# Two attention products made in column halves with 65 moving columns

## The chip, the cores and the metric

The kernel runs on one core of a Trainium2 chip. Its time is the device time of one execution in microseconds (us), and the median of the runs is what counts. The core has five engines: TensorE (PE, which loads a stationary operand of weights and then streams moving columns through the array), VectorE (DVE), ScalarE (ACT), GpSimd (POOL) and SyncE (SP, which issues most DMAs). In the profile, PEld is TensorE's loading of weights.

## The reference

Attention with random features over four batches, eight heads, 576 positions and 64 dimensions, then two feed-forward layers. The change touches the first part alone:

```python
def phi(x):
    proj = np.einsum('bhsd,md->bhsm', x, omega)      # 128 features
    h = proj - np.sum(x * x, axis=-1, keepdims=True) / 2.0
    h = h - np.max(h, axis=-1, keepdims=True)
    return np.exp(h) / np.sqrt(m)
q_p, k_p = phi(q_s), phi(k_s)
kv  = np.einsum('bhsm,bhsd->bhmd', k_p, v)           # values by features
z   = np.sum(k_p, axis=2)
num = np.einsum('bhsm,bhmd->bhsd', q_p, kv)          # numerators
den = np.einsum('bhsm,bhm->bhs', q_p, z)[..., None] + 1e-06
attn = num / den
...
x = (silu(xn @ w_gate) * (xn @ w_val)) @ w_out       # 512 -> 1536 -> 512, xn: attn after an RMS norm
h = x @ w_in
out = (h * np.cos(h)) @ w_out2                       # 512 -> 2048 -> 512
```

## The kernel before

The 2304 tokens are 18 tiles of 128. A batch has four and a half of them, so tiles 4 and 13 are mixed: half of their tokens belong to one batch and half to the next (`parts`, L84).

**Keys.** For a tile, `project` (L419) multiplies the keys of eight heads by omega: contraction over 64 dimensions, two heads side by side in two row halves of the array (L426). `features` (L430) takes the maximum on DVE (L435) and eight exponentials on ACT (L437). `kv_product` (L577) then adds, for each head, features times values: stationary are the 128 features of 128 tokens, moving are 128 columns, of which 64 are the head's values and 64 are ones from an extra block of the tile `v` (slot `H` of `vt`, set by a memset). So the sum of the features, `z`, comes out beside the values. Of the 128 result columns, `keep_kv` (L597) takes 65. A mixed tile is done in two parts of 64 tokens, one after the other, each into its batch's bank.

**Queries.** A query tile goes through eight steps (`query_step`, L707): projection and features; step 1, `transposed` (L440) and `keep_transposed`; step 2, `sums` (L457), the numerators, and `quotients` (L469); then norm, a transpose and a split in a high and a low part. `sums` has the transposed features stationary and 128 columns of `kv` moving, of which 65 are used. A mixed tile needs the sums of two batches: there the stationary operand is cut in two column halves of 64 tokens, and each half gets its own batch's `kv`, with 128 moving columns each.

All these products are fp32. The array runs each fp32 product of the program as two passes, so that one product has two records of a matmul and two of a weight load in the profile. A tile's eight heads are 16 records.

**What sets the order.** The order is written out by hand, in slots. Slot s does, on each engine in this order, what `older` (L765) lists for it and `begin` (L771) adds. In the first stage, up to about 88.8 us, the slots hold 18 key tiles and six query tiles; the weights of the feed-forward layers are prepared in between on ACT, DVE and POOL (`Weights`, L127; `tick`, L363). In the second stage, up to about 262 us, the other twelve query tiles are woven into the first third of the first layer (fp32r products, L831 and L884), and from then on there are feed-forward products only. ACT, DVE and POOL run their lists in the order written too; SP issues the loads of keys, queries, values (L575) and of raw weights, most of them in one queue. The tile `v` has three buffers: the values of tile t + 3 are asked for when tile t's product has been made (L748).

Of the kernel before, what the change touches and what calls it, by code (L numbers as in the profile page):

```python
# [33 lines left out]
F32 = mybir.dt.float32  # L34
# [10 lines left out]
P = 128  # L45
# [11 lines left out]
def attention_then_ffn(ctx: ExitStack, tc: tile.TileContext, qT, kT, v, omT, wc1, rms_g, wc2, out, B, H, S, D):  # L57
    nc = tc.nc
    M = omT.shape[1]
# [12 lines left out]
    C1, C2 = 3, 2  # L72
    RING = 20
    IDLE = 9
    KVW = H * (D + 1) + D
    G = 4
    GROUPS1 = [range(0, 4), range(4, 8), range(8, 12)]
    PER_PAIR = 7
# [5 lines left out]
    def parts(t):  # L84

        pr, i = divmod(t, TPP)
        if i == MIX:
            return [(2 * pr, 0, P // 2), (2 * pr + 1, P // 2, P // 2)]
        return [(2 * pr + (i > MIX), 0, P)]
# [11 lines left out]
    def bank(tag, name):  # L101
        if tag == "w":
            tag = "wa" if w_taken[0] % 2 == 0 else "wb"
            w_taken[0] += 1
        return psum.tile([P, 512], F32, tag=tag, name=name, bufs=2)
# [299 lines left out]
    class Attention:  # L405
# [51 lines left out]
        def sums(self, t, r):  # L457

            eT = self.eT.pop((t, r))
            ps = bank(self.tag, f"num_ps{t}_{r}")  # L460
            for h in range(HP):
                for b, p0, n in parts(t):
                    at = (2 * h + r) * (D + 1)
                    nc.tensor.matmul(
                        ps[p0:p0 + n, h * P:(h + 1) * P], eT[:, h, p0:p0 + n], self.kv[b][:, at:at + P],
                        start=True, stop=True, skip_group_check=True)
            self.ps["num", t, r] = ps

# [76 lines left out]
    with tc.manual_schedule():  # L545
# [16 lines left out]

        kv = [ap.tile([P, KVW], F32, name=f"kv{b}", bufs=1) for b in range(B)]
        NV = 3
        values = ExitStack()
        vp = values.enter_context(tc.tile_pool(name="values", bufs=1, side="right", reuse_waits="tile"))
        vt = [vp.tile([P, H + 1, D], F32, name=f"v{i}", bufs=1) for i in range(NV)]
        att = Attention(att_tile, "q", kv)


        acc = {}

        def load_v(t):
            if t < NTILE:
                nc.sync.dma_start(vt[t % NV][:, 0:H], v[t])  # L575

        def kv_product(t, i):  # L577

            b, p0, n = parts(t)[i]
            end = p0 + n + t * P == (b + 1) * S  # L580
            for r in range(2):
                begin = (b, r) not in acc
                if begin:
                    acc[b, r] = bank("kv", f"kv_ps{b}_{r}")
                for h in range(HP):
                    hh = 2 * h + r
                    nc.tensor.matmul(
                        acc[b, r][:, h * P:(h + 1) * P], att.e["k", t, r][p0:p0 + n, h, :],
                        vt[t % NV][p0:p0 + n, hh::H - hh, :],
                        start=begin and h == 0, stop=end, skip_group_check=True)  # L590
                if end:
                    keep_kv(b, r)
            if i == len(parts(t)) - 1:
                for r in range(2):
                    del att.e["k", t, r]

        def keep_kv(b, r):  # L597
            nc.vector.tensor_copy(
                kv[b][:, 0:H * (D + 1)].rearrange("p (h two d) -> p two h d", two=2, d=D + 1)[:, r],
                acc.pop((b, r)).rearrange("p (h c) -> p h c", c=P)[:, :, 0:D + 1])  # L600
# [143 lines left out]
        for s, (nm, t) in tiles.items():  # L744
# [4 lines left out]
            else:  # L749
                for i in range(1, 8):  # L750
                    at = s + i + (s >= SLOTS - 1 or i > 1)
# [7 lines left out]
        def load_ahead(s):  # L759
            at = order.index(s) if s in tiles else -1  # L760
            if at >= 0 and at + AHEAD[0] < len(order) and at + AHEAD[0] not in asked:
                asked.add(at + AHEAD[0])
                att.load(*tiles[order[at + AHEAD[0]]])

        def older(s, *steps):  # L765
            for step in steps:
                for k, f, *args in then.get(s, []):
                    if k == step:
                        f(*args)

        def begin(s):  # L771
            if s in tiles:
                att.project(*tiles[s])
                for r in range(2):
                    att.features(*tiles[s], r)
# [12 lines left out]
        ps = bank("q", "idle_ps")  # L788
        for _ in range(IDLE):
            nc.tensor.matmul(ps[:, 0:NB], zeros[:, 0:P], zeros, start=True, stop=True)  # L790
        for a in vt:
            nc.vector.memset(a[:, H], 1.0)
        for a in kv:
            nc.vector.memset(a[:, H * (D + 1):], 0.0)
        make_identity(nc, ident)
        nc.gpsimd.memset(half_pi, math.pi / 2)
        nc.gpsimd.memset(minus_half, -0.5)
# [2 lines left out]
        for s in range(SLOTS):  # L800
            load_ahead(s)
            if s in (0, 1):
                load_v(s + 1)
                wts.load(s + 1, nc.sync)
            if s == 3:
                att.load_gain()
            older(s, 0, -5)
            begin(s)
            older(s, -7, -6, -4, -3, -2, -1, 1)
            if s:  # L810
                wts.tick(5 if s < 6 else 1 if s < 14 else 4 if s + 1 < SLOTS else 0)

# [44 lines left out]
        def product(blk, f, e):  # L857
            w = wts.get(1, f, e)
            o = bank("w", f"gv_ps{blk}_{f}_{e}")[:, :NB]
            passes(o, [(two(w, slice(kk * P, (kk + 1) * P)), part(blk, kk)) for kk in range(KD)])  # L860
            return o

        def silu(blk, f, ps):
            a = row(F32, f"gv{blk}_{f}")
            nc.scalar.activation(a, ps, AF.Silu)
            return a
# [10 lines left out]
        def out1(g, blk, f, t, first, last, es):  # L877

            if first and es[0] == 0:
                yacc[blk] = [bank_of_sums(f"y_ps{g}_{blk}_{f}_{e}")[:, :NB] for e in range(KD)]  # L880
            w = wts.get(1, f, 2)
            for i, j in ((0, 0), (1, 0), (0, 1)):
                for e in es:
                    nc.tensor.matmul(yacc[blk][e], w[:, i, e * P:(e + 1) * P], t[:, j],  # L884
                                     start=first and i + j == 0, stop=last and j == 1)
            if not last:
                return
            for e in es:
                waits.append((put_away, blk, e, yacc[blk][e]))
# [59 lines left out]
        for n, (g, blk, f, first, last) in enumerate(steps):  # L949
            tail = n >= N1 - G  # L950
            if tail:
                wts.freed = C1 * f
            back = 2.0 if tail else wts.rate_back(C1 * G + 5, N1 - G - n) / 2
            if wts.n_front < 6 * FRONT:
                back = 0.0
            rates = wts.rate(FRONTS_BY_1, N1 - G + 1 - n) / 2 if n <= N1 - G else 0.0, back
            if n < G:
                rates = max(rates[0], 4), rates[1]
            s = SLOTS + 2 * n
            load_ahead(s)  # L960
            older(s, -5)
            ps = product(blk, f, 0)
            a = silu(blk, f, ps)
            older(s, -6, -4, -3, -2, -1)
            begin(s)
            if n >= 1:
                out1(*steps[n - 1][:3], hid[n - 1], *steps[n - 1][3:], (0, 1))
            older(s, 1, 0)
            job(2 if tail else 3)
            wts.pace(rates[0], 0.0)  # L970
            older(s + 1, -7)
            wts.pace(0.0, rates[1])
            job(0 if tail else 3)
            if n > N1 - G and early_names:
                bring(1, 0, early_names.pop(0))
            flush(3)
            load_ahead(s + 1)
            older(s + 1, -5)
            ps = product(blk, f, 1)
            hid[n] = gated(blk, f, a, ps)  # L980
            older(s + 1, -6, -4, -3, -2, -1)
            begin(s + 1)
            if n >= 1:
                out1(*steps[n - 1][:3], hid.pop(n - 1), *steps[n - 1][3:], (2, 3))
            older(s + 1, 1, 0)
            job(2 if tail else 3)
            wts.pace(rates[0], 0.0)
            older(s + 2, -7)
            wts.pace(0.0, rates[1])
            job(0 if tail else 3)  # L990
            flush(3)
            if n == N1 - G:
                assert s + 2 > max(then)
                while len(combined) < 2:
                    job(1)
                combine.close()
                open_between()
                limit[0] = NPAIR
                tp[:] = [combine.enter_context(tc.tile_pool(name="combinations2", bufs=3, reuse_waits="tile")), 3]
                early_names = ["B11", "B21", "T2", "T1", "T4"]  # L1000
            if n >= N1 - G and early_names:
                bring(1, 0, early_names.pop(0))
# [291 lines left out]
        for k, (g, p) in enumerate(pairs):  # L1294
            fs = list(GROUPS1[g])
            start = base + (g - 1) * PER_GROUP
# [133 lines left out]
```

## Time and profile before

| | us |
|---|---|
| three runs | 964.46, 964.47, 966.03 |
| median | 964.47 |
| profiled execution | 963.77 |
| its span | 961.9 |
| PE busy in the span | 949.2 |
| DVE busy | 712.3 |
| ACT busy | 536.9 |
| POOL busy | 416.4 |

The span is the time from the first to the last instruction of the profiled execution, 1.9 us less than its time. A busy PE is not a PE at its peak, since matmul ends are modelled and overlap. The profile's windows show per stretch how long each engine worked; its timeline shows when a block of equal instructions began and how long it took to the end of the last; its list of waits says who ended an engine's idle time.

### The profile page before, as it was taken

How to read it: one execution, taken by the hardware profiler on the slowest of the kernel's cores; microseconds unless marked ns; L12 is line 12 of the kernel's file. 1: busy time of each engine (PE TensorE's matmuls, PEld its weight loads, DVE VectorE, ACT ScalarE, POOL GpSimd, SP SyncE). 2: the span in 40 equal slices, each digit the busy share in tenths (PEclk: the TensorE clock that was granted, in tenths of full speed). 3: DMA queues.
4: the chain of work that ended last, by engine and by line, in shares of the span. 5: the costliest groups of instructions: out<-in, count | busy, mean ns of one | idle time of the engine just before them, and what ended most of it. 6: DMA issues, size and time to landing. Idle time of an engine off the chain costs nothing. (4 is left out here: it accounts for less than half of the span.)

```text
span 961.9 us, 16225 instructions
## 1 busy us (share of the span) xinstructions
PE 949.2 (99%) x5761; PEld 892.0 (93%) x5761; DVE 712.3 (74%) x1163; ACT 536.9 (56%) x1155; POOL 416.4 (43%) x377
## 2 busy tenths in 40 slices
PE   9999999999999999999999999999999999999998
PEld 8998999989999999999999998888888889899897
DVE  5786677778863686577686648997799777786766
ACT  7787776775543524354453545575656565464443
POOL 2133367657944867275764673320244221230000
PEclk9999999999999999999999999999999999999999
DMA  8555178778697898846989794967622758307554
GB/s 313 157 181 187 57 265 293 256 265 263 219 328 291 328 330 295 302 152 197 376 303 377 249 348 152 345 231 271 208 88 79 272 186 303 125 23 269 197 226 162
DMA packets 96082, 227.65 MB, mean 237 GB/s; under 512 B 9728, under 2 KB 45184, under 8 KB 96000
## 3 DMA queue, kind: packets, MB, share of 16 engines
q1 hardware_dynamic: 94704, 222.34, 66.1%
q10 hardware_dynamic: 1296, 4.26, 1.2%
q8 instruction: 46, 0.75, 0.3%
q14 instruction: 36, 0.29, 0.1%
HBM read 156.04 MB, written 70.52 MB: 236 GB/s over the span
## 5 line engine op out<-in xcount | busy, mean ns | idle before, releaser
L1251 PE MATMUL o_ps<-w,o 128*128 128x512 f32 x864 | 226.0, 393 | 0.6 <-DVE o L1054 0.6
L209 POOL TENSOR_TENSOR f<-f,raw 128x512 f32<-128x512 f32 x68 | 94.7, 1393 | 230.3 <-DVE raw L204 184.6
L1251 PEld LDWEIGHTS o_ps<-w,o 128*128 128x128 f32 x864 | 159.7, 188 | 24.5 <-DVE o L1054 1.1
L217 POOL TENSOR_TENSOR w<-b,w 128x512 fp32r<-128x512 f32 x88 | 115.5, 1318 | 135.4 <-ACT w L214 125.6
L831 PE MATMUL gv_ps<-xhl,w 128*128 128x384 f32 x576 | 107.9, 335 | 1.6 <-DVE gv L870 1.1
L831 PEld LDWEIGHTS gv_ps<-xhl,w 128*128 128x128 f32 x576 | 100.5, 188 | 2.1 <-DVE gv L870 1.4
L1150 PE MATMUL y<-t,w 128*128 128x384 f32 x576 | 102.1, 334 | 0.3 <-POOL w L217 0.3
L1150 PEld LDWEIGHTS y<-t,w 128*128 128x128 f32 x576 | 100.0, 188 | 0.6 <-POOL w L217 0.6
L1051 ACT CAST o<-turns 128x384 fp32r<-128x384 f32 x96 | 47.5, 513 | 93.3 <-DVE turns L1232 93.3
L1043 PE MATMUL Xh<-T,w 128*128 128x384 f32 x432 | 87.4, 337 | 1.5 <-ACT h L1196 1.5
L1043 PEld LDWEIGHTS Xh<-T,w 128*128 128x128 f32 x432 | 76.8, 188 | 9.7 <-ACT h L1196 4.0
L1043 PE MATMUL X<-T,w 128*128 128x384 f32 x432 | 80.9, 335 | 0.0
L1043 PEld LDWEIGHTS X<-T,w 128*128 128x128 f32 x432 | 75.3, 188 | 0.5 <-DVE r L1078 0.3
L214 ACT CAST w<-b 128x512 fp32r<-128x512 f32 x88 | 50.5, 580 | 31.2 <-DVE b L274 23.9
L1054 DVE TENSOR_TENSOR o<-turns,o 128x384 fp32r<-128x384 f32 x96 | 59.9, 638 | 8.5 <-ACT o L1051 8.1
L884 PE MATMUL y_ps<-t,w 128*128 128x384 f32 x288 | 60.8, 346 | 0.0
L1017 ACT ACTIVATE turns<-turns,half_pi 128x768 f32<-128x768 f32 (+1 forms) x50 | 45.7, 914 | 22.4 <-DVE turns L1221 22.3
L1043 PE MATMUL Yh<-B,w 128*128 128x384 f32 x288 | 58.0, 336 | 0.0
L1221 DVE SCALAR_TENSOR_TENSOR turns<-turns,r 128x768 f32<-128x768 int32 (+1 forms) x50 | 56.4, 1128 | 1.7
L1232 DVE TENSOR_TENSOR turns<-h,turns 128x768 f32<-128x768 f32 (+1 forms) x50 | 54.8, 1096 | 2.4 <-ACT turns L1017 2.4
L1043 PEld LDWEIGHTS Yh<-B,w 128*128 128x128 f32 x288 | 51.4, 188 | 4.2 <-ACT h L1196 0.4
L190 DVE TENSOR_SCALAR f<-W 128x512 int32<-128x512 int32 x68 | 45.1, 663 | 13.6 <-ACT W L182 6.5
(117 smaller groups left out, 1853.6 us busy)
## 6 DMA issues: line engine op xcount, KB each, us to landing
T<-T_dram SPq DMA_DIRECT2D x48, 768.0 KB, 6.9
raw<-wc SPq DMA_DIRECT2D x60, 512.0 KB, 4.9
B<-yh_dram SPq DMA_DIRECT2D x21, 768.0 KB, 5.7
kept<-f SPq DMA_DIRECT2D x56, 256.0 KB, 5.0
b<-kept SPq DMA_DIRECT2D x56, 256.0 KB, 5.1
B<-x_dram SPq DMA_DIRECT2D x15, 768.0 KB, 6.6
x_dram<-xhl SPq DMA_DIRECT2D x12, 768.0 KB, 5.8
s<-x_dram SPq DMA_DIRECT2D x24, 384.0 KB, 6.3
```

The lines of the kernel that those rows point to most:

```text
L209: nc.gpsimd.tensor_tensor(f32(f), f32(f), rest, op=ALU.add)
L214: nc.scalar.copy(t[:, 0, to], src)
L217: nc.gpsimd.tensor_tensor(t[:, 1, to], src, f32(t[:, 0, to]), op=ALU.subtract)
L831: nc.tensor.matmul(o, w[i], x[j], start=n == 0, stop=n == len(terms) - 1)
L884: nc.tensor.matmul(yacc[blk][e], w[:, i, e * P:(e + 1) * P], t[:, j], start=first and i + j == 0, stop=last and j == 1)
L1043: nc.tensor.matmul(o, w[:, i, c + kk * P:c + (kk + 1) * P], x[:, j, kk], start=begin and n == 0, stop=n == 5, skip_group_check=True)
L1051: nc.scalar.copy(t[:, 0], a)
L1054: engine.tensor_tensor(t[:, 1], a, f32(t[:, 0]), op=ALU.subtract)
L1150: nc.tensor.matmul(acc[e], w[:, i, e * P:(e + 1) * P], t[:, j], start=f == fs[0] and i + j == 0, stop=f == fs[-1] and j == 1)
L1221: nc.vector.scalar_tensor_tensor(r, a, -TWO_PI_LO, b, op0=ALU.mult, op1=ALU.add)
L1232: at(mu, lambda: nc.vector.tensor_tensor(r, h, r, op=ALU.mult))
L1251: nc.tensor.matmul(oacc[blk][j], o[:, x, js], w[:, y], start=first and n == 0, stop=last and n == 2)
```

## The change

Both products are cut in two column halves: for each head, the 128 columns of the stationary operand become two instructions of 64 columns each, which stand one behind the other and write PSUM partitions 0 to 63 and 64 to 127. The moving operand shrinks from 128 to 65 columns: 64 values and one column of ones for the values by features, 65 columns of `kv` for the numerators. For that the tile `v` gets a layout of eight heads of 65 columns, the 65th a one, in place of eight heads of 64 columns and a block of ones. Its load from memory was a run of 2048 bytes for each token; it is now eight runs of 256 bytes, 260 bytes apart in the tile. The padding of `kv` and its memsets are dropped. The steps 2 and 1 of queries change places in three lists.

```diff
-    KVW = H * (D + 1) + D
+    KVW = H * (D + 1)
...
             for h in range(HP):
-                for b, p0, n in parts(t):
-                    at = (2 * h + r) * (D + 1)
+                at = (2 * h + r) * (D + 1)
+                for c in range(2):
+                    half_c = slice(c * P // 2, (c + 1) * P // 2)
+                    b = parts(t)[min(c, len(parts(t)) - 1)][0]
                     nc.tensor.matmul(
-                        ps[p0:p0 + n, h * P:(h + 1) * P], eT[:, h, p0:p0 + n], self.kv[b][:, at:at + P],
+                        ps[half_c, h * P:h * P + D + 1], eT[:, h, half_c], self.kv[b][:, at:at + D + 1],
                         start=True, stop=True, skip_group_check=True)
...
-        vt = [vp.tile([P, H + 1, D], F32, name=f"v{i}", bufs=1) for i in range(NV)]
+        vt = [vp.tile([P, H, D + 1], F32, name=f"v{i}", bufs=1) for i in range(NV)]
...
-                nc.sync.dma_start(vt[t % NV][:, 0:H], v[t])
+                nc.sync.dma_start(vt[t % NV][:, :, 0:D], v[t])
...
                     hh = 2 * h + r
-                    nc.tensor.matmul(
-                        acc[b, r][:, h * P:(h + 1) * P], att.e["k", t, r][p0:p0 + n, h, :],
-                        vt[t % NV][p0:p0 + n, hh::H - hh, :],
-                        start=begin and h == 0, stop=end, skip_group_check=True)
+                    for c in range(2):
+                        half_c = slice(c * M // 2, (c + 1) * M // 2)
+                        nc.tensor.matmul(
+                            acc[b, r][half_c, h * P:h * P + D + 1], att.e["k", t, r][p0:p0 + n, h, half_c],
+                            vt[t % NV][p0:p0 + n, hh, :],
+                            start=begin and h == 0, stop=end, skip_group_check=True)
...
-            nc.vector.memset(a[:, H], 1.0)
-        for a in kv:
-            nc.vector.memset(a[:, H * (D + 1):], 0.0)
+            nc.vector.memset(a[:, :, D:], 1.0)
...
-            older(s, -7, -6, -4, -3, -2, -1, 1)
+            older(s, -7, -6, -4, -3, -1, -2, 1)
...
-            older(s, -6, -4, -3, -2, -1)
+            older(s, -6, -4, -3, -1, -2)
...
-            older(s + 1, -6, -4, -3, -2, -1)
+            older(s + 1, -6, -4, -3, -1, -2)
```

PE in the first stage, around the first numerators (`num_ps` is their bank, `kv_ps` that of the values by features, `qp_ps` and `kp_ps` those of projections; "x4" are four program instructions in a row), before:

```order
L426 MATMUL qp_ps_1_547<-om,qraw_421 128x128
L464 MATMUL num_ps_0_570<-kv_97,eT_0_498 128x128 x4
L464 MATMUL num_ps_1_580<-kv_97,eT_1_505 128x128 x4
L587 MATMUL kv_ps_0_447<-v_105,ke_0_520 128x128 x4
L587 MATMUL kv_ps_1_452<-v_105,ke_1_527 128x128 x4
L426 MATMUL kp_ps_0_602<-om,kraw_465 128x128
```

and after:

```order
L426 MATMUL qp_ps_1_607<-om,qraw_457 128x128
L466 MATMUL num_ps_0_630<-kv_97,eT_0_550 64x65 x8
L466 MATMUL num_ps_1_644<-kv_97,eT_1_557 64x65 x8
L591 MATMUL kv_ps_0_483<-v_105,ke_0_572 64x65 x8
L591 MATMUL kv_ps_1_492<-v_105,ke_1_579 64x65 x8
L426 MATMUL kp_ps_0_678<-om,kraw_517 128x128
```

Nothing moved: each block stands where it stood, with twice as many instructions of half the stationary and about half the moving columns. The exchange of steps 1 and 2 moves nothing anywhere on any engine, since no slot holds both.

SP at the start of the program, before:

```order
L575 DMA v_104<-v 128x512
L416 DMA kraw_137<-kT 128x512
L170 DMA raw_139<-wc 128x1024
L416 DMA kraw_169<-kT 128x512
L575 DMA v_105<-v 128x512
```

and after:

```order
L577 DMA v_104<-v 128x8x64
L416 DMA kraw_137<-kT 128x512
L170 DMA raw_139<-wc 128x1024
L416 DMA kraw_165<-kT 128x512
L577 DMA v_105<-v 128x8x64
```

The loads keep their places in the queue; only the form of the values' load differs.

## Rows read from the trace of the kernel before

**Rows 1.** The page: busy time and share of each engine, and the chain's engines.

```profile
PE 949.2 (99%) x5761; PEld 892.0 (93%) x5761; DVE 712.3 (74%) x1163; ACT 536.9 (56%) x1155; POOL 416.4 (43%) x377
PE 42%; DVE 3%; ACT 1%; issue 1%; DVEq 0%; ACTq 0%
```

**Rows 2.** Busy time by stretch: its length, then engines, clock, DMA share, GB/s.

```profile
10.00:20.00 10.00, 10.00 (x107) 9.27 (x104) 7.59 (x14) 8.64 (x30) 4.16 (x3) 1.00 0.99 355
6.57:88.84 82.27, 81.17 (x829) 74.70 (x825) 63.11 (x130) 69.21 (x232) 24.87 (x24) 1.00 0.67 221
88.84:262.00 173.16, 170.22 (x1223) 164.90 (x1222) 131.73 (x266) 117.27 (x260) 114.34 (x119) 1.00 0.66 225
```

**Rows 3.** Groups by line and form: records | busy us, mean ns | idle before.

```profile
L587 PE MATMUL kv_ps<-v,ke 128*128 128x128 f32 x256 | 33.0, 282 | 0.3 <-ACT ke L437 0.3
L464 PE MATMUL num_ps<-kv,eT 128*128 128x128 f32 x256 | 31.8, 277 | 0.0
L464 PEld LDWEIGHTS num_ps<-kv,eT 128*128 128x128 f32 x256 | 30.4, 191 | 1.1 <-DVE eT L454 0.3 <-ACT eT L452 0.3
L464 PEld LDWEIGHTS num_ps<-kv,eT 128*64 128x64 f32 x64 | 3.5, 136 | 0.4 <-issue 0.2
```

**Rows 4.** PE's timeline: start, length to the last end (both us), what, records.

```profile
19.75 1.83 PE L587 MATMUL kv_ps<-v,ke 64*128 64x128 f32 x15
...
42.50 2.05 PE L464 MATMUL num_ps<-kv,eT 128*128 128x128 f32 x16
44.39 1.95 PE L587 MATMUL kv_ps<-v,ke 128*128 128x128 f32 x16
46.27 1.16 PE L426 MATMUL kp_ps<-om,kraw 64*128 64x128 f32 x16
...
70.09 4.03 PE L587 MATMUL kv_ps<-v,ke 64*128 64x128 f32 x32
74.05 1.16 PE L426 MATMUL qp_ps<-om,qraw 64*128 64x128 f32 x16
...
85.12 1.98 PE L464 MATMUL num_ps<-kv,eT 128*64 128x128 f32 x32
87.03 2.05 PE L587 MATMUL kv_ps<-v,ke 128*128 128x128 f32 x16
```

**Rows 5.** PEld's timeline in two windows that hold a block's first loads.

```profile
32.45 0.30 PEld L464 LDWEIGHTS num_ps<-kv,eT 128*128 128x128 f32 x2
...
85.12 0.20 PEld L464 LDWEIGHTS num_ps<-kv,eT 128*64 128x64 f32 x4
```

**Rows 6.** PE's timeline in the second stage, numerators between fp32r products.

```profile
97.94 1.95 PE L464 MATMUL num_ps<-kv,eT 128*128 128x128 f32 x16
99.64 1.29 PE L884 MATMUL y_ps<-t,w 128*128 128x384 f32 x6
...
107.29 1.95 PE L464 MATMUL num_ps<-kv,eT 128*128 128x128 f32 x16
109.16 1.16 PE L426 MATMUL qp_ps<-om,qraw 64*128 64x128 f32 x16
```

**Rows 7.** Waits from 6.57 to 88.84 us: total us, times, longest.

```profile
ACT ke L437 <- DVE kmx L435: 10.0, 8, 3.9
ACT qe L437 <- DVE qmx L435: 3.3, 4, 1.8
ACT w L214 <- POOL f L209: 3.0, 4, 1.3
...
DVE kmx L435 <- PE kp_ps L426: 5.3, 5, 2.1
DVE qmx L435 <- PE qp_ps L426: 5.2, 3, 3.3
```

**Rows 8.** PE's longest wait from 89 to 270 us.

```profile
PE gv_ps L831 <- DVE gv L870: 1.1, 1, 1.1
```

**Rows 9.** DMA: ACT's queue from 0 to 6 us (packets, MB, share); loads of values; the fifth one.

```profile
q10 hardware_dynamic: 144, 0.07, 3.8%
...
v<-v SPq DMA_DIRECT2D x18, 256.0 KB, 4.2
...
L575 SPq DMA_DIRECT2D v<-v x1: 327/327/327, 12.4 to 12.4; - x1
...
DMA to landing us min/median/max: 5.7/5.7/5.7
```

## The prediction, made before the result was known

> **What bounds the kernel now.** I read the page first, then the windows by stage, then the timeline of PE around the two products, then the waits. PE is busy 99% of the span, no other engine over 74% [rows 1], so an instruction taken from PE is worth its time, unless the stage where it lies has another engine close behind. That is so in the first stage: from 6.57 to 88.84 us, 82.27 us long, PE works 81.17 us and ACT 69.21 [rows 2]. In the second stage, 173.16 us, PE works 170.22, DVE 131.73 and ACT 117.27: PE alone bounds it [rows 2]. After that there are feed-forward products alone, which the change leaves as they are. All kv products and five of the 18 blocks of numerators lie in the first stage, the other 13 in the second.
>
> **What a block costs PE, and what it will cost.** A block of a whole tile is 16 records. The numerators at 42.50 give way to the next block at 44.39, and that one at 46.27 [rows 4]: 1.88 us, or 0.118 us a record. Streaming is not the only thing of that length. Two weight loads of 128 columns take 0.30 us from the first start to the last end, one takes 0.191 [rows 3, 5], so the second starts 0.11 after the first: loading keeps the same pace as streaming. So 65 moving columns alone would win little; the column halves have to halve the loads too.
>
> The trace has a block of that form: the mixed tile's numerators at 85.12, 32 records of 64 stationary and 128 moving columns, which give way after 1.91 us [rows 4]. That is 0.119 us a pair of halves, no more than one whole record: the two halves stream at once. The loads as well: four half loads (two pairs) span 0.20 us, one takes 0.136 [rows 3, 5], so the fourth starts 0.064 after the first. In single file, at half of 0.11 each, it would be 0.165. A pair of loads therefore costs 0.055, and a pair of streams 65/128 of 0.11, 0.056. I take **0.060 us a pair** (0.055 to 0.075; a pair is four PE instructions, and no row shows four handed out steadily in under 0.11).
>
> The Trainium skill speaks against this: its page "TensorE: Matmul & The Clock Gate", section "The mechanism", says that a weight load overlaps a running matmul only where their row groups differ, and column halves share theirs. By that rule the mixed block would be 16 times 0.055 + 0.11, or 2.6 us, and the changed pair 0.11, with nothing won. The 1.91 us above disagrees, so I give it no more than the weight of the first rival.
>
> So a block falls by 16 x (0.118 - 0.060) = 0.93 us, less what the pipeline needs to start and drain, which does not shrink: I take 0.83.
> - First stage, kv of 16 whole tiles: 13.3 us.
> - First stage, kv of two mixed tiles: each has two blocks of 16 records of 64 tokens, one behind the other, 3.96 us for 32 [rows 4]; now 32 pairs, 1.9. Together 4.1 us.
> - First stage, five numerators: 4.2 us. The mixed one is among them, with 0.119 a pair before.
> - Second stage, 13 numerators: these stand between whole products, and a change of tiling has a price. A block of them followed by whole products gives way after 1.70 us, one followed by the row-halved projection after 1.87 [rows 6]: 0.17 a change. The changed block needs 16 x 0.058 + 2 x 0.17 = 1.27. It is eight times followed by a projection (0.60 won) and five times not (0.43): 7.0 us.
>
> PE is freed of 21.6 us in the first stage and 7.0 us in the second.
>
> **What of it shows in the end.** First stage: PE's work would fall to 59.6 us, ACT's stays at 69.2. ACT becomes the bound. It sits idle for 13.1 us there, and that alone can be won. Of it, 9.4 us are waits for DVE's maxima (10.0 + 3.3, less the first 3.9, which ends at 6.57), and 3.0 for POOL [rows 7]. DVE in turn waits 10.5 us for projections [rows 7], which come sooner now, but it also has weight work of its own in front of some maxima. I take two thirds of 9.4: **6 us**, between 3 and 9.4. What is late next is ACT itself, and behind it DVE with 63.11 us.
>
> The values' load takes some of it back. It is not shown in pieces of 256 bytes. DMA is 0.99 busy from 10 to 20 us at 355 GB/s [rows 2], 22.4 bytes a ns for each of 16 engines, so a piece of 2048 takes 91 ns; 512-byte pieces, omega's, take 0.038 x 16 x 6 us / 128 = 28 ns [rows 9]. A straight line through both gives 17.5 ns for 256 bytes; the upper end is 28, as much as for 512. A load of 1024 pieces is 64 an engine: 1.1 to 1.8 us against 0.73, 0.4 to 1.06 more. I take 0.73, the middle. DMA is saturated when the first five are fetched, so it adds up: the fifth is issued at 12.39 and lands 5.7 us later, at 18.1, and PE wants it at 19.75 [rows 4, 9]. With five times 0.73 it lands at 21.7: **2 us** lost (0.3 to 3.6). Later loads have two slots of over 2.5 us each from issue to use, against a median landing of 4.2 [rows 9]; no loss.
>
> On transfers the Trainium skill speaks against the change too: its page "DMA: Bandwidth & Descriptors", section "Specifications", wants 512 bytes or more a piece for full speed and says that smaller ones are read, modified and written back. No row here shows a load of that size; by that rule the sum is near that of the third rival.
>
> Second stage: 7.0 us freed. PE waits little there, its longest wait is 1.1 us for DVE [rows 8], but DVE works 76% and will have less room: I take 70%, **5 us** (3 to 7). The smaller memsets (seven before, three now) and the exchanged steps cost nothing: they move nothing that PE waits for.
>
> Sum: 963.8 - 6 + 2 - 5 = 954.8 for the profiled execution. It lies 0.7 below the median, so **955.5 us**.
>
> **The rivals.**
> 1. The pair does not shrink: loads or the handing out of four instructions keep it at 0.11. For it: no row shows a pair faster. Against: the loads' starts [rows 5]. Nothing is won and the load of values costs 0.3 to 2 us: 965 us.
> 2. All of it shows: ACT loses all 9.4 us of waits, the second stage wins all 7.0, and values are not late: 963.8 - 16.4 + 0.7 = 948. For it: DVE's 10.5 us of waits for PE. Against: ACT's waits for POOL and DVE's own work remain.
> 3. Slower: small pieces cost more than the line says. Over the first stage DMA is 0.67 busy, 55 us [rows 2]; 18 loads add 18 x (0.064 c - 0.73) us at c ns a piece. DMA then takes as long as the stage did, plus the 5 us that the second stage wins, at 18 x 1.8 = 32 us more, or c = 39 ns. If a piece is fetched twice over (35 to 56 ns, in the middle 45), the first stage takes 55 + 38.7 = 93.7 us, 11.4 more than before, less 5: 971 us. Against it: 28 ns at 512 bytes.
> 4. The clock falls, since PE now pauses in every slot of the first stage. It was granted at 1.00, 2.4 GHz, in every stretch [rows 2], but PE never paused there. At half the clock, 1.2 GHz, for half of its work there, PE's 59.6 us become 89.4, 7.1 more than the stage takes now: 963.8 + 7.1 + 2 - 5 + 0.7 = 969 us.
>
> **How the numbers follow.** The forecast has 0.61, with its own range of 949 to 962 from the bounds above; rival 2 has 0.17, rival 1 0.10, rival 3 0.08, rival 4 0.04. The range takes in the first two rivals, 945 to 965 us, and leaves out the last two and a little at its lower end. A measurement of this kernel tells about 0.2% from no change, 962.5 to 966.4: faster 0.78, same 0.10, slower 0.12.
>
> **What would show it.** In the profile after: a block of 32 records of 64 by 65 that gives way after 0.95 to 1.2 us; PE busy in the first stage some 60 us, with waits for ACT and its exponentials where there were none; ACT over 90% busy there; the fifth load of values landing near 21.7 and the product of that tile waiting for it; the second stage shorter by 3 to 7 us; all later stages as long as before. The forecast is wrong if blocks stay near 1.9 us (rival 1), if PE waits for values throughout (rival 3), or if later stages give the gain back, for which no row speaks.

## The result and the profile after

| | before, us | after, us |
|---|---|---|
| median | 964.47 | 955.16 |
| lowest and highest of four runs | 964.16, 966.03 | 953.72, 956.19 |
| profiled execution | 963.77 | 955.29 |
| its span | 961.9 | 953.5 |

The ratio of the two kernels' times is 0.9899, with a 95% interval of 0.9882 to 0.9916: 9.7 us faster by the ratio, 9.3 by the medians. The forecast was 955.5. It came out of terms that were off on both sides, as the experiments show; so the profile first, part by part.

The page of after, first busy time and then the chain, beside [rows 1]:

```profile
PE 929.5 (97%) x6337; PEld 866.7 (91%) x6337; DVE 713.4 (75%) x1159; ACT 537.1 (56%) x1155; POOL 415.5 (44%) x377
PE 43%; DVE 3%; ACT 1%; issue 1%; DVEq 0%; ACTq 0%
```

PE worked 19.7 us less in a span that is 8.4 us shorter: over half of what PE was freed of, 11.3 us, became idle time. The groups of the two products, beside [rows 3]: records, then busy us and mean ns, then idle time before:

```profile
L591 PE MATMUL kv_ps<-v,ke 128*64 128x65 f32 x512 | 21.2, 228 | 1.8 <-DMA v<-v 1.6
L466 PE MATMUL num_ps<-kv,eT 128*64 128x65 f32 x576 | 20.8, 225 | 0.7 <-DVE eT L454 0.7
```

PE's timeline in the first stage, beside [rows 4] (start and length in us, what, records, and in brackets the idle time before it and its releaser):

```profile
13.85 2.04 PE L591 MATMUL kv_ps<-v,ke 128*64 128x65 f32 x32 [0.96 <-DMA v<-v]
15.81 1.16 PE L426 MATMUL kp_ps<-om,kraw 64*128 64x128 f32 x16
17.61 1.47 PE L591 MATMUL kv_ps<-v,ke 128*64 128x65 f32 x32 [0.64 <-DMA v<-v]
...
39.77 1.15 PE L466 MATMUL num_ps<-kv,eT 128*64 128x65 f32 x32
40.75 1.30 PE L591 MATMUL kv_ps<-v,ke 128*64 128x65 f32 x32
...
65.91 2.23 PE L591 MATMUL kv_ps<-v,ke 64*64 64x65 f32 x64 [0.57 <-DVE kv L602]
68.08 1.44 PE L426 MATMUL qp_ps<-om,qraw 64*128 64x128 f32 x16
```

The numerators at 39.77 give way after 0.98 us; the same block at 42.50 before took 1.89. The two batches of a mixed tile are done in 2.17 us where it was 3.96. The rows at 13.85 and 17.61 show the price: PE waits for values, 1.6 us in all. The block at 13.85 also keeps PE until 15.81, 1.96 us; such blocks count as busy while they wait inside for the second half of the exponentials.

Busy time by stretch, beside [rows 2] (length, then PE, PEld, DVE, ACT, POOL, clock, DMA share, GB/s). The first product of gates and values, which ended the first stage at 88.84 before, now starts at 82.04:

```profile
6.57:82.04 75.47, 66.12 (x1221) 57.26 (x1217) 63.35 (x126) 67.35 (x228) 25.41 (x24) 1.00 0.84 242
82.04:253.50 171.46, 166.00 (x1418) 157.36 (x1415) 133.11 (x271) 118.63 (x265) 112.59 (x119) 0.98 0.66 227
```

The first stage is 6.80 us shorter. PE now idles 9.35 us in it (1.1 before). ACT idles 8.1 us (13.1 before), which makes 4.9 of the 6.8; the other 1.9 is ACT work that before lay in the first stage (69.21 us) and now lies behind its end (67.35). The clock of the second stage is 0.98; it was 1.00 in both stages before [rows 2]. The waits from 6.57 to 82.04, first ACT's, then DVE's, beside [rows 7] (total us, times, longest):

```profile
ACT ke L437 <- DVE kmx L435: 7.7, 7, 4.3
ACT w L214 <- POOL f L209: 2.8, 4, 1.0
ACT qe L437 <- DVE qmx L435: 0.9, 2, 0.7
...
DVE kmx L435 <- PE kp_ps L426: 4.0, 3, 2.2
DVE f L190 <- ACT W L182: 4.0, 2, 3.1
DVE qmx L435 <- PE qp_ps L426: 2.3, 2, 1.6
```

DVE waits 6.3 us for projections instead of 10.5, so the maxima are there sooner. ACT's waits for maxima, less the first one, fell from 9.4 us to 4.3. The wait for POOL stayed.

The second stage, where [rows 6] stood before:

```profile
91.65 1.15 PE L466 MATMUL num_ps<-kv,eT 128*64 128x65 f32 x32
92.74 1.34 PE L886 MATMUL y_ps<-t,w 128*128 128x384 f32 x6
...
100.53 1.15 PE L466 MATMUL num_ps<-kv,eT 128*64 128x65 f32 x32
101.61 1.16 PE L426 MATMUL qp_ps<-om,qraw 64*128 64x128 f32 x16
```

Counted from the product ahead of each block to the product behind it, and where nothing waits, 0.70 us is won where a projection follows and 0.47 where it does not: 8 x 0.70 + 5 x 0.47 = 8 us are freed. They are not all kept. At the product that started at 201.88 us before, after is 10.0 us ahead: of the 5.6 us that nine blocks have freed by then, 3.2 show. Between 159 and 167 us alone 1.8 are lost, 1.0 of them in three waits of PE. At the product of 273.10 after is only 8.0 ahead. What happens between is in PE's timeline of after, then in DVE's:

```profile
197.52 1.03 PE L444 MATMUL eT_ps<-ident,qe 128*128 128x128 f32 x8
200.32 0.46 PE L426 MATMUL qp_ps<-om,qraw 64*128 64x128 f32 x2 [1.76 <-issue]
201.20 2.07 PE L426 MATMUL qp_ps<-om,qraw 64*128 64x128 f32 x14 [0.43 <-DVE gv L872]
203.21 2.29 PE L886 MATMUL y_ps<-t,w 128*128 128x384 f32 x6
205.29 3.37 PE L833 MATMUL gv_ps<-xhl,w 128*128 128x384 f32 x12
208.59 1.15 PE L466 MATMUL num_ps<-kv,eT 128*64 128x65 f32 x32
```

```profile
194.84 0.69 DVE L204 SCALAR_TENSOR_TENSOR raw<-raw 128x512 f32<-128x512 uint32 x1
199.13 0.43 DVE L190 TENSOR_SCALAR f<-W 128x512 int32<-128x512 int32 x1 [3.60 <-ACT W L184]
199.47 0.75 DVE L518 TENSOR_TENSOR xhl<-xT_ps,xhl 128x256 fp32r<-128x256 f32 x2
```

The projection at 200.32 needs a bank that DVE's split (L518) has to empty. The split stands behind a weight step (L190) that waits 3.60 us for ACT, so PE pauses 1.76 us. Then three blocks take 2.07, 2.29 and 3.37 us instead of 1.16, 1.31 and 2.24 as elsewhere, 3.0 us more: the granted clock is down to 1.2 GHz, half of 2.4. In the kernel before, the same DVE step waited 3.62 us for ACT, and PE paused there too:

```profile
209.50 0.46 PE L426 MATMUL qp_ps<-om,qraw 64*128 64x128 f32 x2 [0.93 <-PE eT_ps L444]
```

So the pause costs 0.8 us more than it did before, the slow blocks 3.0. Some of it comes back at PE's wait of 1.1 us for DVE [rows 8], which is gone in after. The windows around the fall:

```profile
198.00:201.00 3.00, 1.01 (x8) 0.61 (x5) 1.87 (x5) 1.46 (x4) 2.83 (x5) 0.98 0.99 352
201.00:204.00 3.00, 2.80 (x16) 2.58 (x17) 2.42 (x5) 2.35 (x4) 2.84 (x4) 0.50 0.69 227
204.00:207.00 3.00, 3.00 (x11) 3.00 (x11) 2.97 (x5) 3.00 (x10) 2.84 (x4) 0.50 0.30 119
207.00:210.00 3.00, 3.00 (x42) 2.68 (x41) 1.06 (x4) 1.34 (x2) 2.76 (x3) 0.88 0.51 183
```

The loads of values in after, beside [rows 9]: what SP needs to issue one (ns: least, median, most), and the time to landing (us):

```profile
L577 SPq DMA_DIRECT2D v<-v x18: 540/546/1217, 1.6 to 68.2; - x18
...
DMA to landing us min/median/max: 3.3/4.4/7.3
```

### The profile page after: what moved, and what is told of

Same layout as the page of the kernel before. It is cut to its first block, busy times and chain, and to the rows that moved or that the text cites. A ratio compares the mean times of both kernels' runs of the same rounds, so it can differ in the third digit from the quotient of the medians.

```text
span 953.5 us, 17373 instructions
## 1 busy us (share of the span) xinstructions
PE 929.5 (97%) x6337; PEld 866.7 (91%) x6337; DVE 713.4 (75%) x1159; ACT 537.1 (56%) x1155; POOL 415.5 (44%) x377
## 5 line engine op out<-in xcount | busy, mean ns | idle before, releaser
L190 DVE TENSOR_SCALAR f<-W 128x512 int32<-128x512 int32 x68 | 44.0, 647 | 15.1 <-ACT W L182 6.5
```

## The experiments

Each was timed beside the kernel before (median 964.7 to 965.5 us); ratios are to those runs. How far the traces are ahead (negative) or behind the kernel before, at the starts of three products and in the span:

| | product of 88.84 | of 201.88 | of 273.10 | span | ratio of times, 95% interval |
|---|---|---|---|---|---|
| after | -6.8 | -10.0 | -8.0 | -8.4 | 0.9899, 0.9882 to 0.9916 |
| e1, halves, 128 columns | +0.3 | +2.7 | +2.7 | +4.2 | 1.0012, 1.0002 to 1.0021 |
| e2, whole, 65 columns | +4.7 | +4.3 | +5.1 | +5.1 | 1.0079, 1.0053 to 1.0105 |
| e3, pieces alone | +1.0 | +1.7 | +1.7 | +2.5 | 1.0019, 1.0005 to 1.0033 |
| e4, numerators alone | -3.5 | -7.6 | -6.8 | -6.8 | 0.9922, 0.9902 to 0.9942 |
| e5, values alone | -1.0 | -0.3 | -0.3 | -0.6 | 0.9962, 0.9950 to 0.9975 |
| e6, one run, strided | -1.7 | -5.9 | -5.0 | -4.4 | 0.9944, 0.9929 to 0.9959 |
| e7, split first | -4.0 | +0.5 | +4.6 | +5.1 | 1.0024, 1.0012 to 1.0036 |
| e8, e6 and e7 | -2.0 | +2.5 | +6.6 | +6.4 | 1.0058, 1.0041 to 1.0075 |
| e9, ones in memory | -7.4 | -11.1 | -10.2 | -9.8 | 0.9880, 0.9866 to 0.9894 |
| e10, first stage alone | -5.9 | -4.7 | -4.7 | -5.0 | 0.9941, 0.9925 to 0.9957 |
| e11, one step later | -4.5 | -8.7 | -7.0 | -6.9 | 0.9897, 0.9881 to 0.9914 |
| e12, e9 and e11 | -7.2 | -11.2 | -9.6 | -9.7 | 0.9889, 0.9873 to 0.9904 |

The ratios come from four to ten executions of each kernel, the other columns from one trace each, and one trace tells the first stage only to some 3 us. After, e7, e10 and e11 are the same code up to the product of 88.84, and their traces are 6.8, 4.0, 5.9 and 4.5 us ahead there. In them PE waits 1.6, 4.0, 0.9 and 3.7 us for values, and the clock falls to 1.2 GHz for 3.4 us twice in that stage of e7 and once in that of e11.

**Which part saves the time: loads or columns?** e1 has both products in halves, but with 128 moving columns; e2 has whole stationary operands with 65.

```diff
# e1, beside after (both products); the values' layout and load are those of before
-   ps[half_c, h * P:h * P + D + 1], eT[:, h, half_c], self.kv[b][:, at:at + D + 1],
+   ps[half_c, h * P:(h + 1) * P], eT[:, h, half_c], self.kv[b][:, at:at + P],
# e2, from before (both products; shown: numerators), with the values' layout and load of after
-   ps[p0:p0 + n, h * P:(h + 1) * P], eT[:, h, p0:p0 + n], self.kv[b][:, at:at + P],
+   ps[p0:p0 + n, h * P:h * P + D + 1], eT[:, h, p0:p0 + n], self.kv[b][:, at:at + D + 1],
```

> The kernel before, with both products cut in column halves as in the change, but with 128 moving columns as before and the old load of values. Theory: halves load and stream at once, so that a pair takes as long as a whole record did. Blocks of numerators and of values by features still give way after 1.8 to 2.0 us, and the time is 964 to 967 us (the upper end if the change of tiling around the 13 numerators of the second stage costs 0.2 us each). Rival: the halves are themselves what wins (loads of 64 columns no longer hold back the stream), blocks under 1.6 us and a time under 961. Second rival: halves in single file, blocks of 3.5 us, 1000 us or more.

> The changed kernel with whole stationary operands: 128 columns at once (64 only where a mixed tile needs it), 65 moving columns, values loaded in 256-byte pieces. Theory: loading 128 columns keeps the pace at 0.11 us a record, so that a block of 16 still gives way after 1.7 to 1.9 us; nothing won but for the mixed tile's numerators, some 0.3 to 2 us lost to the values: 964 to 967 us. Rival: streaming alone is the bound, blocks near 1.0 us as in the changed kernel, and 955 us.

Neither gains; e1 does what its theory said. Its blocks of halves with 128 columns take 1.80 and 1.85 us, as in PE's timeline of e1:

```profile
43.13 1.97 PE L466 MATMUL num_ps<-kv,eT 128*64 128x128 f32 x32
44.93 1.92 PE L591 MATMUL kv_ps<-v,ke 128*64 128x128 f32 x32
46.78 1.16 PE L426 MATMUL kp_ps<-om,kraw 64*128 64x128 f32 x16
```

In e2 a block of 65 columns still takes 1.88 us:

```profile
57.03 1.95 PE L587 MATMUL kv_ps<-v,ke 128*128 128x65 f32 x16
58.91 1.16 PE L426 MATMUL kp_ps<-om,kraw 64*128 64x128 f32 x16
...
71.60 4.61 PE L587 MATMUL kv_ps<-v,ke 64*128 64x65 f32 x32
```

So loading sets the pace there, streaming in e1, and only both together halve it. e2 lost 8 us in the median, more than either theory gave. Its profiled execution is the fastest of its five, 968.82 us, with a span 5.1 us longer than before. In it, e2 is 1.5 us behind the kernel before at the start of that last block, a mixed tile, and 5.9 at 85.31. PE's windows show why: PE is busy all the time, and the clock is at 1.2 GHz:

```profile
74.60:79.00 4.40, 4.40 (x29) 4.06 (x29) 0.74 (x2) 1.20 (x4) 1.99 (x3) 0.51 0.86 236
79.00:84.90 5.90, 5.90 (x36) 5.56 (x36) 3.23 (x7) 3.03 (x11) 0.00 (x0) 0.50 0.74 259
```

The other four executions of e2, of 972.66 to 976.08 us, have mean clocks of 0.985 to 0.991, against 0.994 in this one: PE worked longer at 1.2 GHz in them. No trace shows where.

**The price of the small pieces, and each product alone.** e3 is the kernel before with only the layout of `v` and its load changed; e4 has the change in the numerators alone, e5 in the values by features (with layout and load) alone.

```diff
# e3, from before
-   vt = [vp.tile([P, H + 1, D], F32, ...
+   vt = [vp.tile([P, H + 1, D + 1], F32, ...
-   nc.sync.dma_start(vt[t % NV][:, 0:H], v[t])
+   nc.sync.dma_start(vt[t % NV][:, 0:H, 0:D], v[t])
-   vt[t % NV][p0:p0 + n, hh::H - hh, :],
+   vt[t % NV][p0:p0 + n, hh::H - hh, 0:D],
# e4, from before: of the change, the loop of sums alone
+   for c in range(2):
...
+       ps[half_c, h * P:h * P + D + 1], eT[:, h, half_c], self.kv[b][:, at:at + D + 1],
# e5, from before: of the change, the loop of kv_product, vt and load_v
+   for c in range(2):
...
+       acc[b, r][half_c, h * P:h * P + D + 1], att.e["k", t, r][p0:p0 + n, h, half_c],
+       vt[t % NV][p0:p0 + n, hh, :],
```

> The kernel before with one edit: the values are loaded in 256-byte pieces, 260 bytes apart, as in the change; products as before. Theory: 1024 pieces of about 18 ns take 0.4 to 0.5 us longer than 128 of 84 ns, which adds up over the first five loads; the product of the third or fourth tile waits for them, and the time is 1 to 2 us longer: 965.5 to 966.5. Rival: hidden behind the wait for ACT, 964 to 965.

> The kernel before with the numerators alone changed (column halves, 65 moving columns); values by features and their load as before. Theory: 5 blocks of the first stage win about 0.9 us each, of which most shows since ACT has room when only they are shorter (3 to 4.5 us); the second stage wins what it won in the changed kernel, 1.5 to 2 us, the rest of its 8 us going into longer waits for DVE; nothing is lost to late values: 958 to 960 us. Rival: what the second stage won there was cut by its starting 6.8 us earlier than its weights are ready; it then wins 5 us or more here, and the time is 955 to 957.

> The kernel before with the values by features alone changed (column halves, 65 moving columns, values loaded in 256-byte pieces); numerators as before. PE is freed of some 17 us, all in the first stage. Theory: ACT bounds that stage once PE is shorter, so that the two halves of the change don't add up: alone, this one wins 4.5 to 6 us by the end of the stage, more than the 3.3 us that the changed kernel has over the numerators alone (6.8 against 3.5), and nothing later: 959 to 960.5 us. Rival: they add up, the stage ends 3.3 us earlier and the time is 961.5 to 962.5.

e3 lost 1.0 us in the first stage and 1.8 by the ratio, 1.4 in the median: the pieces alone cost that. e4, after with the values by features as before, won 7.5 us by the ratio: 3.5 up to the end of the first stage, the rest in the second. A block of the first stage wins 0.70 to 0.90 us there, 3.8 in all; a wait of 0.5 us takes some of it back, and the trace was 0.3 ahead before the first block. It beat its theory because the second stage kept 3.3 us and not 2; its rival's 5 were not reached. e5 won 3.7, and the time is its rival's. But the rival's path, a first stage 3.3 us shorter, is not in the trace, which is of the slowest of six executions: that stage is only 1.0 us shorter, and the clock falls twice in it, for 3.4 us each. Alone the two products win 7.5 and 3.7 us, 11.2 together, where the whole change wins 9.7; the difference is within the intervals. PE waits longer for values in e5 than in after, about as long as in e7 and e11, as the chief entry of its list of waits up to 83 us shows:

```profile
PE kv_ps L589 <- DMA v<-v: 4.0, 4, 1.5
```

**Can the pieces be avoided?** e6 puts the heads innermost, so that a token is one run of 2048 bytes; its moving columns then lie 32 bytes apart. e9 keeps the layout of after and has the ones in memory beside the values.

```diff
# e6, from after
-   vt[t % NV][p0:p0 + n, hh, :]
+   vt[t % NV][p0:p0 + n, :, hh]
# e9, from after: v comes as [..., H, D + 1], its last column ones
-   nc.sync.dma_start(vt[t % NV][:, :, 0:D], v[t])
+   nc.sync.dma_start(vt[t % NV], v[t])
-   nc.vector.memset(a[:, :, D:], 1.0)
```

> The changed kernel with the values laid out by dimension and head in memory and in the tile, so that a token's values are again one run of 2048 bytes, the ones are the last eight columns, and the 65 moving columns of a head lie 32 bytes apart. Theory: the late values cost the changed kernel 1.6 us of PE's waits and about 2 us of the first stage; now no product waits for values, the stage ends about 8.5 us before that of the kernel before (6.8 in the changed kernel), and the time is 953 to 954.5 us. Rival: moving columns 32 bytes apart stream slower; blocks of values by features over 1.3 us, the gain is lost, 955 us or more.

> The changed kernel, with the ones stored in memory beside the values, so that a token's eight heads of 65 columns come as one run of 2080 bytes and the memsets of ones are gone. The moving columns stay one behind the other, the blocks stay as they are. My theory: the pieces of 256 bytes make the first values late and cost the first stage 1.0 to 1.6 us; without them PE's waits for values between 10 and 20 us (0.96 and 0.64 in the changed kernel) are gone, the first stage is 7.5 to 8.5 us shorter than before instead of 6.8, and 0.5 to 1.5 of that is left at the end: 953.7 to 954.7 us. Rival: the stage is paced by the exponentials' chain of maxima, so the early loss is caught up anyway: the same time as the changed kernel, 955.2, within 0.5 us.

In e6 PE no longer waits for values, but the block takes 2.05 us, more than before the change, as its rival said:

```profile
10.21 2.12 PE L591 MATMUL kv_ps<-v,ke 128*64 128x65 f32 x32
12.26 1.16 PE L426 MATMUL kp_ps<-om,kraw 64*128 64x128 f32 x16
```

Columns 32 bytes apart stream at half the pace. e9 has neither trouble: 953.43 us (952.17 to 955.03), 1.7 under the changed kernel and a little more than its theory said, though the two intervals overlap. Against after's trace only 0.6 us is won in its first stage: PE waits 1.3 us for the exponentials instead of 1.6 for values, and in the profiled execution the clock fell for 3.4 us at 15.8. Against the four traces with the same first stage, 5.3 us ahead on average, e9 and e12 win 2.0 us with 7.4 and 7.2. e9 is the shortest kernel of this study.

**What is left of the second stage's 8 us?** e10 is the changed kernel with whole numerators in the second stage (and, not shown, the padding of `kv` that they need).

```diff
+   if self.tag == "w":
+       ...          # L457 to L467 of the kernel before
+   else:
        ...          # L461 to L468 of after
```

> The changed kernel with the numerators of the second stage whole again (128 stationary and 128 moving columns, as in the kernel before); those of the first stage and all values by features stay in halves. My theory: of the 8 us that the halved blocks free in the second stage only 1.2 to 1.6 last to its end, so this kernel loses no more than that: the first stage 6.8 us shorter than before, the second as long as before, 956.3 to 958.5 us. Rival: the halved blocks are worth the 5 us that I forecast, and the fall of the clock took them away in the profiled execution only: 960 us and more.

958.99 us, between the two theories. By the ratios, 0.9941 and 0.9899, the first stage's part is 5.7 us and the second stage's halves are 4.0; by the intervals the one is known to 1.5 us either way, the other to 2.2. The table shows one more thing: with the second stage as it was, e10 still falls back by 1.2 us in it. In this trace a shorter first stage gives part of its gain back there. That fits the 1.9 us of ACT work pushed behind its end, but no run took that work away.

**What takes the rest?** e7 moves DVE's split (L518) ahead of the weight steps in every slot of the second stage; e8 is e6 and e7 together.

```diff
# e7, from after, in both halves of a step
-   wts.pace(rates[0], 0.0)
    older(s + 1, -7)
+   wts.pace(rates[0], 0.0)
```

> The changed kernel with one order changed: in the second stage, DVE's low parts of a query tile's transpose (which free the bank that the next projection waits for) stand ahead of the weight steps of that slot, not behind them. Theory: the gain of the 13 numerators is lost where PE waits for that bank (1.8 us at 200.3 us, 0.4 at 160.8, 0.5 at 219.2), behind a DVE step that waits 3.6 us for ACT; after the longest of these pauses the granted clock was 0.50 for 6.8 us, which cost another 1 to 2 us. Now these waits go, the clock stays at 1.00, and the second stage wins 4 to 6 us instead of 1.2: 951 to 953.5 us. Rival: DVE and ACT as a whole bound these slots, the wait comes back at the next step, and the time stays at 954.5 to 956.

> The changed kernel with both edits of the two runs before: values in one run of 2048 bytes, and the low parts ahead of the weight steps. Theory: the two losses lie in different stages and add up: 950 to 952 us. Rival: what the first stage wins earlier is given back in the second, whose waits are for DVE and ACT: 952 to 954.

Both got slower than the kernel before, and than their theories. The wait only changed its place: the split now waits itself for ACT's half of it, with the weight steps behind it. DVE's timeline of e7 at the longest of these waits, then its list of waits from 82 to 272 us, first after's line and then e7's:

```profile
127.00 0.76 DVE L518 TENSOR_TENSOR xhl<-xT_ps,xhl 128x256 fp32r<-128x256 f32 x2 [3.19 <-ACT xhl L516]
...
DVE xhl L518 <- ACT xhl L516: 4.6, 4, 2.5
DVE xhl L518 <- ACT xhl L516: 12.1, 6, 3.2
```

e11 then moves one weight step alone, at the pause of 200 us, behind the products; e12 has that and e9's loads.

```diff
# e11, from after
-   wts.pace(rates[0], 0.0)
+   if n != 12:
+       wts.pace(rates[0], 0.0)
    older(s + 1, -7)
    ...
    hid[n] = gated(blk, f, a, ps)
+   if n == 12:
+       wts.pace(rates[0], 0.0)
```

> The changed kernel with one edit at one place of the second stage: at step 12 of the first layer, where PE of the changed kernel pauses 1.76 us (198.6 to 200.3) because DVE's split of the tile stands behind a weight step that waits 3.60 us for ACT, that weight step is issued after the products of gates and values of that step. My theory: the pause is what brings the clock to half from 200.9 to 207.7; DVE's split then ends near 198.7, PE pauses about 0.1 us and then 0.5 for the next bank, the clock stays at 1.00 from 198 to 213 us, and the kernel is 1.5 to 4 us shorter: 951.5 to 954. Rival: the fall comes from the narrow blocks themselves, pause or not, or another pause takes its place: the clock falls near 200 us or a little later all the same, 954.5 us or more.

> Both edits: ones stored in memory beside the values (one run of 2080 bytes a token) and the one weight step after the products at step 12. My theory: they add up, since one works on the first 20 us and the other near 200 us: 1.7 us from the first and 1.5 to 4 from the second, 949.5 to 952 us, the shortest yet. Rival: the stage's end is set by DVE's and ACT's lists, which are no shorter, so the one gain eats the other: 953 us or more, as with the stored ones alone.

The pause and the fall behind it are gone, in both. PE's timeline and window of e11 at that place:

```profile
200.16 0.46 PE L426 MATMUL qp_ps<-om,qraw 64*128 64x128 f32 x2 [0.24 <-PE eT_ps L444]
201.04 1.16 PE L426 MATMUL qp_ps<-om,qraw 64*128 64x128 f32 x14 [0.43 <-DVE gv L872]
...
201.00:204.00 3.00, 2.69 (x22) 2.25 (x23) 2.44 (x5) 2.85 (x4) 1.19 (x1) 1.00 0.87 308
```

But the time did not move: e11 has 955.02 us (954.91 to 956.78), e12 954.54 (954.03 to 955.24). The pause went as the theory said, and the gain did not come. That the pause brings the fall is not shown: e4 has the same pause, 1.74 us at 202.7, and no fall. In e11's profiled execution, the slowest of its five, the clock fell for 3.4 us at 80.8 instead. And in both, what was won at 200 us is given back later. The first lines of e12's list of PE's waits from 190 to 275 us, where the kernel with the pause has none longer than 0.7 besides it:

```profile
PE qp_ps L426 <- DVE xhl L518: 1.5, 1, 1.5
PE gv_ps L831 <- DVE gv L870: 1.4, 1, 1.4
```

e12 had no fall of the clock before its last microseconds, e9 had two, and their spans are 952.2 and 952.1. So the rival of e12 holds. I read it so: in the second stage DVE's list, woven with ACT's, sets how far PE can get ahead, some 10 us by its end, and what one place saves, the next wait for DVE takes. That the waits come back is shown; that no other order of those lists would do better is not.

## Why the prediction came out right

1. **The pair of halves.** Forecast 0.060 us; the numerators at 39.77 took 0.98 / 16 = 0.061. The two half streams and the half loads run at once, as the mixed block of [rows 4, 5] had shown. The Trainium skill, "TensorE: Matmul & The Clock Gate", section "The mechanism", lets a weight load overlap a running matmul only where row groups differ, which would leave 0.11; the traces disagree with 0.061. Rival 1 is out. That loads keep the pace of 128 columns, so that 65 columns alone win nothing, is shown by e2; that halves with 128 columns win nothing, by e1.
2. **A block wins 0.83.** A block of the first stage won 0.70 to 0.90 in e4, one of the second 0.70 or 0.47 (0.60 or 0.43 forecast): 8 us freed there against 7.0. This was a little low in the second stage and near in the first. The 0.17 us that I read off [rows 6] as the price of a change of tiling does not hold: in [rows 4] a block followed by whole products took 1.89 as well, and the changed blocks gave way after 1.09 and 1.08 in front of either kind, where I had 1.27.
3. **What ACT gives back in the first stage.** Forecast 6 of 9.4 us of waits for maxima; 5.1 went. The stage still shrank by 6.8, because 1.9 us of ACT's weight work moved behind its end. The step that failed is that I held ACT's work in the stage at 69.2 us. PE worked 66.1 us in it, not 59.6, in part because blocks that wait inside count as busy.
4. **Late values.** Forecast 2 us (0.3 to 3.6), out of 0.73 a load. PE waited 1.6 us in after and 0.9 to 4.0 in the traces with the same first stage; e3 puts the stage's loss at 1.0, and e9 and e12 are 2.0 ahead of the average of those four traces. So the size holds, within a wide spread. The price of a load was too high: a piece of 256 bytes took 18 ns in after's trace, one of 2048 84 ns (medians), which makes 64 x 18 - 8 x 84 = 480 ns a load. The place was off: the third and fourth tiles waited, not the fifth, whose values landed near 20.0 us, just before its product at 20.18. The rival of pieces fetched twice over, 971 us, is out. The Trainium skill, "DMA: Bandwidth & Descriptors", section "Specifications", which wants 512 bytes or more a piece, points the right way: 256 bytes in 18 ns are 14 bytes a ns, 2048 in 84 are 24. By its read, modify and write, as rival 3 worked it out, the stage would have become 11.4 us longer; e3's 1.0 us doesn't show that.
5. **The first stage in sum.** Forecast -6 + 2 = -4; by e10 it is worth 5.7 at the end (4.1 to 7.2 by the interval). Under-sized by 1.7.
6. **The second stage.** Forecast 5 of 7.0 (70% kept); by e10 against after 4.0 of 8, half. Over-sized by 1, though the 5 lies within the interval. I had named DVE as what would be late next, rightly. What I had not seen is the form: a split queued behind a weight step that waits for ACT, and the clock that falls behind PE's pause.
7. **The clock.** Rival 4 was right that the clock would fall and wrong in size and place. It forecast half of the first stage's work at 1.2 GHz; in after's trace it was 6.8 us in the second stage, 3.0 us lost there, and in the first stage of e7 and e11 3.4 us at a time. PE had paused in the first stage before as well, once for 0.67 us near 84, without a fall. Rival 2, that all shows, fails twice: 5.1 of 9.4 us of waits went, and 4.0 of 8 us showed.

So 1.7 too little and 1 too much nearly cancelled, and that the forecast lies 0.3 us from the measured median is luck. The range would have held either alone.

## What to carry to other kernels

Where an fp32 product's stationary operand has 128 columns and few moving ones, cut both, as here: columns alone leave the loads as the bound, halves alone the streams. Before counting the gain, ask of each stage which engine is next, and follow one bank from the engine that waits to the instruction at the head of the emptying engine's list: over half of what PE was freed of ended as idle time, much of it in waits for lists that were no shorter. When a layout is changed to suit PE, keep the moving columns side by side and the memory side in long runs at once; e9 did so by storing the ones with the values.

## What the hardware did that I had not expected

- **Falls of the clock to 1.2 GHz**, for 3.4 us in most cases, 6.8 in after and 10.2 in e2, before the last microseconds of the span, in the profiles of after and of e2, e5, e6, e7, e8, e9 and e11; none in those of before, e1, e3, e4, e10 and e12. Shortly before all but e2's, PE had paused, for 0.97 us (e9) to 2.24 (e7), 1.76 in after. In e2 PE had not paused; the fall began 3 us into the block of 71.60, which loads 64 rows by 128 columns and streams 65. A pause is not enough: e4 has the same one of 1.7 us near 202 us, and its clock stayed at 1.00; the pause of 1.6 us near 80 us has a fall behind it in e5, e7 and e11 and none in after, e9, e10 and e12. Executions of one kernel differ too: after's four, of 953.72, 955.03, 955.29 and 956.19 us, have mean clocks of 0.998, 0.998, 0.996 and 0.996. What decides is open.
- **Moving columns 32 bytes apart** take twice as long: 2.05 us a block in e6, where columns side by side take some 1.1.
- **Small pieces cost SP too**: 0.546 us to issue a load of 1024 pieces in after, 0.328 for the 128 runs of e9 (medians).
- **A late load far behind the change:** e1 and e3 lose a further 1.6 and 0.8 us after the second stage, where they do not differ from the kernel before. Of it, 1.4 and 0.5 go at one product near 360 us, where PE waits for DVE, which has waited 3.5 us for a load of `y` from memory (2.5 in the kernel before). Why the load was later is open.
